# Turning the tokens of single batches with VectorE blocks and small transfers instead of TensorE

## The chip, the core and the metric

The kernel runs on one core of a Trainium2 chip. The metric is the device time of one execution in microseconds. Before the change the median of three runs is 2033.48 us (2031.84 to 2034.04).

The engines go by the profile's names: PE is TensorE, DVE is VectorE, ACT is ScalarE, POOL is GpSimd, SP is SyncE. SP and POOL matter here only as queues that issue transfers; each queue issues in program order, and each engine runs its instructions in program order.

## The reference

```python
# x: 8 batches x 4096 tokens x 192 channels; 8 heads of 24 channels, 7 taps
w    = softmax(weight, axis=-1)                    # 8 x 7
conv = sum over k of w[head, k] * x[token - 6 + k] # causal, per head
# mixing over tokens: w_tok1 4096x256, w_tok2 256x4096
h = relu(conv.T @ w_tok1) @ w_tok2
u = conv + h.T
# mixing over channels: w_ch1 192x1536, w_ch2 1536x192
out = u + relu(u @ w_ch1) @ w_ch2
```

The kernel does each matrix product as three products of a high and a low part (`hi*hi + hi*lo + lo*hi`), so each operand has to be split: the high part is a rounded copy, the low part is the value minus the high part.

## The kernel before, in words

The batches are worked in five groups, `[0], [1], [2, 3], [4, 5], [6, 7]`: two single batches, then three pairs. A batch's 4096 tokens are worked in 8 tiles of 512 (four columns `j` of 128). While group g's tiles go through the channel products, the background prepares group g+1: its convolution on DVE (line 659, six taps behind a first tap on ACT, line 657) and its first token product on PE (lines 761 for singles, 765 to 767 for pairs), whose sum over all 4096 tokens has to be complete before the next group's first tile can be formed.

One tile runs so on PE:

- **channel 1** (`channel1_mm`, line 1012): 6 steps of 18 matmuls. Each reads the turned tokens (channels on partitions), `own_hi` and `own_lo`. ACT (1051) and DVE (1052) turn each result into the pair `hh`, `hl`.
- **token mix** for the *next* tile (`mix2`, lines 909 and 910 for singles, 912 to 914 for pairs). DVE adds the results to the convolved tokens in `u` (922, 923; for pairs 927).
- **channel 2** (lines 1086, 1087): 4 columns of 24 matmuls, each closed by two DVE adds (1092, 1093) into `osb`.

The next tile's tokens stand token by row and have to be turned before its channel 1. For **single** batches PE does it, in the middle of channel 2 (`transposed`, line 945: 12 transposes of 128x128 against an identity, from a doubled copy of the tokens that ACT makes at line 924), and ACT (947) and DVE (948) split the result from PSUM. For **pairs** the work goes around PE: DVE turns each column in 32x32 blocks as soon as it is mixed (928) into a buffer `z` that takes the slot of `own_hi`; 16 transfers of 48 KB (`blocks_sent`, 961), eight from SP's queue and eight from POOL's, put the blocks in their places; and in the third column of channel 2, after its eighth of twelve steps, ACT and DVE split what arrived (`parted`, 974 and 976).

The order is set by a planner, `Background`. It keeps estimated clocks for PE and DVE. Each foreground step adds its estimate (`bg.fg(pe, dve)`), and background items are placed while the estimated DVE is not ahead of the estimated PE by more than a margin. Items also have gates: the first tap on a loaded chunk waits until the load should have landed. Between `bg.hold()` and `bg.release()` the convolution's big loads and stores are kept back, so that the small transfers go ahead of them; `bg.behind` adds 5 us to what is released. Before a group's last tile, `bg.finish` writes out everything of the next group's preparation that is not yet placed; PE's remaining token product stands there, ahead of the last tile's channel 1.

## Time and profile before

| | us |
|---|---|
| median of three runs | 2033.48 |
| the profiled execution | 2034.48 |
| its span, first to last instruction | 2032.7 |
| PE busy | 2019.6 |
| DVE busy | 1452.2 |
| ACT busy | 761.7 |
| POOL busy | 220.3 |

In the trace the tiles of batch 0 take PE from 62 to 335 us, those of batch 1 to 608 us, and the rest are pairs. A tile is told by its first line-1012 matmul: batch 0's second tile starts at 101.66 us, its last at 305.04 us, batch 1's first at 335.04 and its last at 577.96 us. "Busy" of PE counts from an instruction's start to its modelled end, and matmuls overlap, so PE's cost of a stretch is read here from the start of one group of matmuls to the start of the next.

### The profile page before, as it was taken

To read this page: it belongs to the slowest core of one execution; us is meant where nothing else is said; L and a number is where in the kernel's file an instruction comes from. 1 tells how busy PE (TensorE), PEld (TensorE's weight loads), DVE (VectorE), ACT (ScalarE), POOL (GpSimd) and SP (SyncE) were. 2 spreads that over 40 slices of the span, in tenths; PEclk is the share of its full clock that TensorE was granted. 3 is DMA by queue.
4 is the path that set the end of the run, shared out by engine and by line. 5 is a ranking of instruction groups with operands and counts; after the bars stand their busy time and mean duration, and the time that the engine had idled before them with its cause. 6 is when DMAs were issued, how large, how long until landed. Compare 5 with 4: busy or idle time off the path is not lost.

```text
span 2032.7 us, 42017 instructions
## 1 busy us (share of the span) xinstructions
PE 2019.6 (99%) x17435; PEld 1857.9 (91%) x17435; DVE 1452.2 (71%) x2877; ACT 761.7 (37%) x1305; POOL 220.3 (11%) x383
## 2 busy tenths in 40 slices
PE   9999999999999999999999999999999999999999
PEld 9789999999999898999999999999999999999998
DVE  7899998999659998756986689545555545555554
ACT  4575544444433434233333334233222332233322
POOL 0100000000011011101111110111111011111110
PEclk9999999999999999999999999999999999999999
DMA  9855346454434567324654334533222233233310
GB/s 304 294 158 170 119 155 201 152 163 157 142 117 131 165 200 202 101 82 130 169 162 114 106 107 137 150 89 84 71 61 57 71 84 84 76 84 84 84 48 17
DMA packets 289230, 258.39 MB, mean 127 GB/s; under 512 B 209360, under 2 KB 238544, under 8 KB 289040
## 3 DMA queue, kind: packets, MB, share of 16 engines
q1 hardware_dynamic: 265120, 168.00, 29.2%
q0 software_dynamic: 23920, 87.71, 14.0%
q8 instruction: 138, 2.26, 0.5%
q14 instruction: 52, 0.43, 0.1%
HBM read 146.60 MB, written 71.30 MB: 107 GB/s over the span
## 4 chain that ended last, share of the span: by engine, by line
PE 88%; DVE 5%; DMA 4%; SPq 1%; ACT 1%; issue 1%; POOL 0%; DVEq 0%; ACTq 0%
PE ps_x L1012 36%; PE ps_x L1086 17%; PE ps_x L1069 15%; PE ps_x L1087 8%; PE ps_x L912 2%; PE ps_a L765 2%; DVE xc L659 2%; PE ps_a L767 2%; PE ps_a L766 2%; PE ps_x L914 2%; PE ps_x L913 2%; PE ps_x L909 1%; PE ps_x L945 1%; PE ps_a L761 1%; DMA dec_raw<-in_moe_w_ch_dram 1%; DVE hl L1052 1%
## 5 line engine op out<-in xcount | busy, mean ns | idle before, releaser
L1051 ACT ACTIVATE hh<-ps_x 128x512 fp32r<-128x512 f32 x756 | 410.9, 596 | 743.3 <-PE ps_x L1012 743.2
L1052 DVE SCALAR_TENSOR_TENSOR hl<-ps_x,hh 128x512 fp32r<-128x512 f32 x756 | 484.5, 685 | 198.0 <-ACT hh L1051 196.6
L1086 PE MATMUL ps_x<-w,hh 128*128 128x384 f32 x1872 | 538.3, 359 | 0.1
L1087 PE MATMUL ps_x<-w,hl 128*128 128x192 f32 x1872 | 468.6, 250 | 0.0
L1012 PE MATMUL ps_x<-other,w_hi 64*128 64x512 f32 x1728 | 450.2, 389 | 1.0 <-DVE osb L1093 0.9
L659 DVE SCALAR_TENSOR_TENSOR xc<-raw,cw,xc 128x384 f32<-128x384 f32 (+1 forms) x768 | 389.2, 562 | 9.8 <-ACT xc L657 9.8
L1087 PEld LDWEIGHTS ps_x<-w,hl 128*128 128x128 f32 x1872 | 357.4, 191 | 0.0
L1086 PEld LDWEIGHTS ps_x<-w,hh 128*128 128x128 f32 x1872 | 351.4, 188 | 0.7 <-DVE hl L1052 0.7
L1012 PEld LDWEIGHTS ps_x<-other,w_hi 64*128 64x128 f32 x1728 | 314.0, 184 | 32.6 <-issue 1.3
L1012 PE MATMUL ps_x<-own_hi,w_hi 64*128 64x512 f32 x1440 | 333.6, 393 | 1.6 <-DVE hl L1052 0.9
L1069 PE MATMUL ps_x<-w,hh 64*128 64x384 f32 x2304 | 329.8, 355 | 0.0
L1012 PE MATMUL ps_x<-own_hi,w_lo 64*128 64x512 f32 x1440 | 325.4, 387 | 0.0
L1012 PE MATMUL ps_x<-own_lo,w_hi 64*128 64x512 f32 x1440 | 325.3, 386 | 0.0
L1069 PE MATMUL ps_x<-w,hl 64*128 64x192 f32 x2304 | 294.0, 247 | 0.0
L1012 PEld LDWEIGHTS ps_x<-own_hi,w_hi 64*128 64x128 f32 x1440 | 209.6, 184 | 37.8 <-issue 6.2
L1012 PE MATMUL ps_x<-other,w_lo 64*128 64x512 f32 x864 | 242.0, 386 | 0.0
L1012 PEld LDWEIGHTS ps_x<-own_hi,w_lo 64*128 64x128 f32 x1440 | 215.2, 184 | 29.1 <-DVE w_lo L212 0.5
L1012 PEld LDWEIGHTS ps_x<-own_lo,w_hi 64*128 64x128 f32 x1440 | 215.4, 184 | 28.1
L1069 PEld LDWEIGHTS ps_x<-w,hl 64*128 64x128 f32 x2304 | 229.0, 188 | 1.1 <-DVE hl L1052 0.2
L1069 PEld LDWEIGHTS ps_x<-w,hh 64*128 64x128 f32 x2304 | 225.2, 184 | 0.9
L1012 PEld LDWEIGHTS ps_x<-other,w_lo 64*128 64x128 f32 x864 | 159.0, 184 | 16.0
L1092 DVE TENSOR_TENSOR osb<-ps_x,u 128x192 f32<-128x192 f32 x156 | 55.4, 355 | 144.3 <-PE ps_x L1087 143.7
(143 smaller groups left out, 2153.2 us busy)
## 6 DMA issues: line engine op xcount, KB each, us to landing
raw<-in_x_dram SPq DMA_DIRECT2D x56, 672.0 KB, 7.5
t<-t2d SPq DMA_DIRECT2D x64, 512.0 KB, 5.4
out_dram<-osb POOLq DMA_DIRECT2D x63, 384.0 KB, 4.6
u<-xcd SPq DMA_DIRECT2D x62, 384.0 KB, 6.6
xcd<-xc POOLq DMA_DIRECT2D x28, 768.0 KB, 7.5
t<-t1p SPq DMA_DIRECT2D x32, 512.0 KB, 4.9
other<-own_hi SPq DMA_DIRECT2D x192, 48.0 KB, 2.1
other<-own_hi POOLq DMA_DIRECT2D x192, 48.0 KB, 2.0
```

The lines of the kernel that those rows point to most:

```text
L659: nc.vector.scalar_tensor_tensor(out=dst, in0=src, scalar=cw[:, h, k:k + 1], in1=dst, op0=ALU.mult, op1=ALU.add)
L765: nc.tensor.matmul(out=ps, lhsT=wh, rhs=xh, start=a, stop=False)
L766: nc.tensor.matmul(out=ps, lhsT=wh, rhs=xl, start=False, stop=False)
L767: nc.tensor.matmul(out=ps, lhsT=wl, rhs=xh, start=False, stop=z)
L912: nc.tensor.matmul(out=ps[:, :n], lhsT=wh, rhs=hh, start=a, stop=False)
L1012: nc.tensor.matmul(out=ps, lhsT=w1[w][rows, c, p * P:(p + 1) * P], rhs=t[h][v][rows, c], start=n == 0, stop=n == len(prods) - 1,)
L1051: nc.scalar.activation(out=h["hh", f], in_=ps, func=AF.Relu)
L1052: nc.vector.scalar_tensor_tensor(out=h["hl", f], in0=ps, scalar=0.0, in1=f32(h["hh", f]), op0=ALU.max, op1=ALU.subtract)
L1069: nc.tensor.matmul(out=ps[:, :m], lhsT=h[part, f][ks, ts], rhs=w2[ks, f, :m], start=n == 0 and part == "hh", stop=z and part == "hl",)
L1086: nc.tensor.matmul(out=ps[:, :2 * D], lhsT=h["hh", f][:, ts], rhs=w2[:, f, :], start=n == 0, stop=False)
L1087: nc.tensor.matmul(out=ps[:, :D], lhsT=h["hl", f][:, ts], rhs=w2[:, f, :D], start=False, stop=z)
L1092: nc.vector.tensor_tensor(out=rows(osb[:, j]), in0=rows(ps[:, :D]), in1=tokens(u, i)[:, j], op=ALU.add)
```

## The change

For the turns to tiles 3 to 8 of batch 0 and to all eight tiles of batch 1 (14 turns) the single batches take the way of the pairs, with some differences:

- `u` holds a tile's two copies one behind the other (`flat`), not alternating by 64 channels. DVE adds both as before and then turns the mixed copy by 32x32 blocks into `z` (new line 938). The copy on ACT (924), the 12 transposes on PE (945) and the split from PSUM (947, 948) are gone for these turns.
- The 16 transfers write into the slot of `own_lo` itself. Rows 64 to 127 get the same channels as rows 0 to 63, so every block is sent twice.
- `parted_single`: ACT writes the high part in the tokens' true order (998); DVE subtracts in place (1004), and the low part stays in the order in which the blocks arrived. Channel 1 reads it through a permuted view, in runs of 32 elements.
- Loads and stores of the convolution are held from channel 1's third step on, and a held load of a single batch now counts the 5 us of `bg.behind`.

```diff
             else:
                 mark("load", q2, part)
+                done["load", q2, part] += bg.behind
...
+            elif turned is not None and nb == 1:
+                two, one = flat(u)[:, j, 0], flat(u)[:, j, 1]
+                nc.vector.tensor_tensor(out=one, in0=ps[:, :D], in1=one, op=ALU.add)
+                nc.vector.tensor_tensor(out=two, in0=ps[:, D:2 * D], in1=one, op=ALU.add)
+                nc.vector.transpose(
+                    out=turned[:, :D // QB, j * QB:(j + 1) * QB], in_=two.rearrange("p (n e) -> p n e", e=QB)
+                )
+                bg.dve += 380
...
+        if nb == 1:
+            other = own_tile("lo")
+            blocks = z[:, :D // QB].rearrange("p (c n) t -> p n c t", n=NQ // 2)
+            home = other
...
                 queue.dma_start(
-                    out=f32(other[q * QB:(q + 1) * QB, 1, :, i * P:(i + 1) * P]), in_=blocks[i * QB:(i + 1) * QB, q]
+                    out=f32(home[q * QB:(q + 1) * QB, :, i * P:(i + 1) * P]),
+                    in_=blocks[i * QB:(i + 1) * QB, q % (2 * nb)],
                 )
...
+    def parted_single(lo):
+        own = own_tile("hi")
+        for c in range(ND):
+            v = f32(lo[:, c])
+            nc.scalar.copy(
+                out=own[:, c].rearrange("p (j i e) -> p j i e", i=NQ, e=QB),
+                in_=v.rearrange("p (i j e) -> p j i e", i=NQ, e=QB),
+            )
+            bg.fg(0, 700, 0)
+            blocks = "p (i j e) -> p i j e"
+            nc.vector.tensor_tensor(
+                out=lo[:, c].rearrange(blocks, i=NQ, e=QB), in0=v.rearrange(blocks, i=NQ, e=QB),
+                in1=f32(own[:, c]).rearrange("p (j i e) -> p i j e", i=NQ, e=QB), op=ALU.subtract,
+            )
+        own = own, lo.rearrange("p c (i j e) -> p c j i e", i=NQ, e=QB)
+        return [(own, own)]
...
         for p in range(NP):
+            if p == hold:
+                bg.hold()
...
-                if turn and pairs:
-                    bg.hold()
+                by_blocks = turn and (pairs or ahead)
                 if ahead:
-                    h = channel1(abc[i])
+                    h = channel1(abc[i], (0 if pairs else 2) if by_blocks else None)
...
+                    if by_blocks:
+                        other = blocks_sent(z, len(GROUPS[nxt[0]]))
+                        bg.release()
                 if ahead:
                     product2(i, h, u, osb, half[0])
-                if turn and not pairs:
+                if turn and not by_blocks:
                     abc = transposed(loaded[1])
...
-                        if turn and pairs:
+                        if by_blocks:
                             made = []
-                            channel2(i, h, u, osb, half[1], ((half[1][0], 7), lambda: made.extend(parted(other))))
+                            split = parted if pairs else parted_single
+                            channel2(i, h, u, osb, half[1], ((half[1][0], 7), lambda: made.extend(split(other))))
```

The planner's sums change with it, so the background stands elsewhere. The first place is DVE at the end of channel 2 of batch 0's seventh tile, where `bg.finish` writes out the rest of batch 1's preparation. `xc` and `raw` are the convolution's result and input, `h` is the finished first token product. Before:

```order
L1092 TENSOR_TENSOR osb<-ps_x,u 128x192
L1093 TENSOR_TENSOR osb<-ps_x,osb 128x192
L948 TENSOR_TENSOR own_lo<-ps_x,own_hi 128x512 x3
L1092 TENSOR_TENSOR osb<-ps_x,u 128x192
L1093 TENSOR_TENSOR osb<-ps_x,osb 128x192
L1092 TENSOR_TENSOR osb<-ps_x,u 128x192
L1093 TENSOR_TENSOR osb<-ps_x,osb 128x192
L382 SCALAR_TENSOR_TENSOR h_486<-ps_a_759,h_486 128x192
```

With the change:

```order
L1139 TENSOR_TENSOR osb<-ps_x,u 128x192
L1140 TENSOR_TENSOR osb<-ps_x,osb 128x192
L659 SCALAR_TENSOR_TENSOR xc_3164<-raw_2855,cw,xc_3164 128x8x24 x12
L1004 TENSOR_TENSOR own_lo<-own_lo,own_hi 128x512 x3
L659 SCALAR_TENSOR_TENSOR xc_3164<-raw_2855,cw,xc_3164 128x8x24 x2
L1139 TENSOR_TENSOR osb<-ps_x,u 128x192
L1140 TENSOR_TENSOR osb<-ps_x,osb 128x192
L659 SCALAR_TENSOR_TENSOR xc_3164<-raw_2855,cw,xc_3164 128x8x24 x2
L659 SCALAR_TENSOR_TENSOR xc_3164<-raw_3151,cw,xc_3164 128x8x24 x10
L1139 TENSOR_TENSOR osb<-ps_x,u 128x192
L1140 TENSOR_TENSOR osb<-ps_x,osb 128x192
L659 SCALAR_TENSOR_TENSOR xc_3164<-raw_3151,cw,xc_3164 128x8x24 x14
```

Before, batch 1's convolution was complete a tile earlier and PE's last 16 line-761 matmuls stood inside the seventh tile's token mix; now 14 taps stand behind the tile's last add, and those 16 matmuls stand between the tile's channel 2 and the last tile's channel 1.

The second place is DVE at the end of channel 2 of batch 1's seventh tile, where the rest of the first pair's preparation is written out. `xhl` is the split convolution result that PE multiplies, `t` and `other` the split first token weight (`other` is a spare buffer). Before:

```order
L749 TENSOR_TENSOR xhl<-xc_5281,xhl 128x768
L1092 TENSOR_TENSOR osb<-ps_x,u 128x192
L1093 TENSOR_TENSOR osb<-ps_x,osb 128x192
L733 TENSOR_TENSOR other<-other 128x2x256
L749 TENSOR_TENSOR xhl<-xc_5281,xhl 128x768
L733 TENSOR_TENSOR other<-other 128x2x256
L749 TENSOR_TENSOR xhl<-xc_5281,xhl 128x768
L382 SCALAR_TENSOR_TENSOR h_486<-ps_a_3724,h_486 128x384
```

With the change (the last four pairs of lines 734 and 750 are cut to one):

```order
L1139 TENSOR_TENSOR osb<-ps_x,u 128x192
L1140 TENSOR_TENSOR osb<-ps_x,osb 128x192
L659 SCALAR_TENSOR_TENSOR xc_5938<-raw_5923,cw,xc_5938 128x16x24 x20
L750 TENSOR_TENSOR xhl<-xc_5148,xhl 128x768
L734 TENSOR_TENSOR t_6207<-t_6207 128x2x256
L750 TENSOR_TENSOR xhl<-xc_5938,xhl 128x768
```

Twenty taps now stand behind the last add, and in front of five of the six splits that PE's remaining product of 72 matmuls (48 before) waits for; the first of the six was made earlier. From the end of this flush on, DVE's rows are the same in both kernels to the end of the program.

More of the change, by code (lines that the diff above doesn't have):

```diff
@@ L949, in transposed, with blocks_sent @@
         return [(own, own)]
-    def blocks_sent(z):
-        other = sp.tile([P, 2, ND, TT], F32R, name="other")
-        blocks = z.rearrange("p (c n) t -> p n c t", n=NQ)
+    def blocks_sent(z, nb):
+        if nb == 1:
+            other = own_tile("lo")
+            blocks = z[:, :D // QB].rearrange("p (c n) t -> p n c t", n=NQ // 2)
+            home = other
+        else:
+            other = sp.tile([P, 2, ND, TT], F32R, name="other")
+            blocks = z.rearrange("p (c n) t -> p n c t", n=NQ)
+            home = other[:, 1]
         for k in range(NQ):
@@ L1037, in conv_mixer_kernel, with channel1 @@
     order = [p + h * NP for p in range(NP) for h in range(2)]
-    def channel1(t):
+    def channel1(t, hold):
         h = {}
@@ L1243, in conv_mixer_kernel @@
                     first_channel2(u, osb, half[0])
-                if turn and pairs:
-                    z = up.tile([P, ND * NQ, P], F32, name="own_hi")
-                    mix2(*nxt, *loaded, turned=z)
-                    other = blocks_sent(z)
-                    bg.release()
-                elif turn:
+                if turn:
                     if gi == 0 and nxt[0] == 0:
                         bg.require(("t2", nxt[1] // 2, nxt[1] % 2))
-                    mix2(*nxt, *loaded)
+                    z = up.tile([P, ND * NQ, P], F32, name="own_hi") if by_blocks else None
+                    mix2(*nxt, *loaded, turned=z)
                     mixed[0] = nxt[1]
+                    if by_blocks:
+                        other = blocks_sent(z, len(GROUPS[nxt[0]]))
+                        bg.release()
                 product2 = channel2 if turn or last and q + 1 == NT and i + 1 == nb else channel2_halves
```

12 lines of the change are left out of this document (10 added, 2 removed).

## The prediction

> **What bounds the kernel now.** I read the page's shares and slices first, then the chain of waits, then the busy times by stretch over the single batches.
>
> ```profile
> span 2032.7 us, 42017 instructions
> PE 2019.6 (99%) x17435; PEld 1857.9 (91%) x17435; DVE 1452.2 (71%) x2877; ACT 761.7 (37%) x1305; POOL 220.3 (11%) x383
> DVE  7899998999659998756986689545555545555554
> PE 88%; DVE 5%; DMA 4%; SPq 1%; ACT 1%; issue 1%; POOL 0%; DVEq 0%; ACTq 0%
> ```
>
> PE is busy 99% of the span and is 88% of the chain: whatever leaves PE shortens the time, as long as nothing makes PE wait. The last row is DVE's busy tenths in 40 slices: in the first twelve, where the change acts, it stands at 7 to 9 for the most part.
>
> ```profile
> 275.00:300.00 25.00, 24.90 (x179) 22.92 (x177) 24.79 (x52) 9.19 (x20) 0.55 (x1) 1.00 0.27 94
> 550.00:575.00 25.00, 25.00 (x170) 24.92 (x169) 14.16 (x30) 9.29 (x17) 2.60 (x5) 1.00 0.38 127
> ```
>
> Each row is a stretch; the columns are its length, then busy time of PE, PEld, DVE, ACT, POOL, the granted clock (1.00, full), DMA share and GB/s. At the end of batch 0 DVE is busy 24.79 of 25 us and PE still 24.90; at the end of batch 1 DVE has 11 us to spare in 25. So DVE is nearly a second bound while batch 0 runs, and only the planner's early finish of the convolution keeps it off PE.
>
> **What PE sheds.** PE's rows of one single tile, from the first channel-2 matmul to the next channel 1, and the same stretch in a tile that turns a pair by blocks:
>
> ```profile
> 349.86 0.36 PE L1086 MATMUL ps_x<-w,hh 128*128 128x384 f32 x1
> 356.69 1.47 PE L945 MATMUL ps_x<-ident,u 128*128 128x128 f32 x12
> 357.92 0.42 PE L1086 MATMUL ps_x<-w,hh 128*128 128x384 f32 x1
> 365.04 0.97 PE L1012 MATMUL ps_x<-own_hi,w_hi 64*128 64x512 f32 x6
> ...
> 594.72 0.33 PE L1086 MATMUL ps_x<-w,hh 128*128 128x384 f32 x1
> 608.44 0.49 PE L1012 MATMUL ps_x<-own_hi,w_hi 64*128 64x512 f32 x1
> ```
>
> The 12 transposes hold PE from 356.69 to 357.92, 1.23 us. The whole stretch takes 15.18 us with them and 13.72 without, 1.46 less: changing operations costs something too. I take 1.35, between the two. Fourteen turns give 18.9 us (17.2 to 20.4). One stall goes as well:
>
> ```profile
> PE ps_x L1012 <- DVE osb L1093: 0.9, 1, 0.9
> ```
>
> It is DVE's backlog before batch 0's seventh tile, where the order now has fewer taps: 0.9 us. Gain: 19.8.
>
> **What the new way costs.** First the rows for its operations (groups by line and shape; of the transfers, the issue durations as min/median/max in ns):
>
> ```profile
> L928 DVE STREAM_TRANSPOSE own_hi<-u 128x384 f32<-128x384 f32 x96 | 55.6, 579 | 3.3
> L961 SPq DMA_DIRECT2D other<-own_hi x192: 589/597/1987, 596.8 to 1970.1; - x192
> L961 POOL DMA_DIRECT2D other<-own_hi x192: 548/548/586, 597.4 to 1969.2; - x192
> L976 DVE TENSOR_TENSOR own_lo<-other,own_hi 128x512 fp32r<-128x512 f32 x72 | 45.5, 687 | 40.6 <-ACT own_hi L974 37.4 <-DMA t<-t2d 3.2
> ```
>
> The turn of 192 columns isn't in the trace. It lies between half the 384-column turn, 0.29, and the whole, 0.58; I take 0.41, near the middle: 1.6 us more of DVE per tile. The subtraction is priced by the pairs' row, 0.69, and takes the place of one of the same shape; ACT sheds four copies, which nothing waits for once they are gone. Eight issues of 0.60 on SP run beside eight of 0.55 on POOL: 4.8 us until the last is out. Behind them in SP waits the held convolution load.
>
> **When the turned tokens are ready.** The rows of a token mix and turn, single and pair:
>
> ```profile
> 317.50 0.44 PE L909 MATMUL ps_x<-h,t 128*128 128x384 f32 x1
> 318.24 1.29 DVE L1052 SCALAR_TENSOR_TENSOR hl<-ps_x,hh 128x512 fp32r<-128x512 f32 x2 [0.69 <-ACT hh L1051]
> 319.45 0.35 DVE L922 TENSOR_TENSOR u<-ps_x,u 128x192 f32<-128x192 f32 x1
> 319.86 0.36 PE L1086 MATMUL ps_x<-w,hh 128*128 128x384 f32 x1
> 320.11 0.35 DVE L922 TENSOR_TENSOR u<-ps_x,u 128x192 f32<-128x192 f32 x1
> ...
> 596.12 0.58 DVE L928 STREAM_TRANSPOSE own_hi<-u 128x384 f32<-128x384 f32 x1
> 604.05 1.67 ACT L974 CAST own_hi<-other 128x512 fp32r<-128x512 f32 x3 [12.43 <-DMA other<-own_hi]
> 604.71 1.90 DVE L976 TENSOR_TENSOR own_lo<-other,own_hi 128x512 fp32r<-128x512 f32 x3 [2.24 <-ACT own_hi L974]
> ```
>
> Count from the first mix matmul. DVE begins the adds at 1.95 (319.45 − 317.50) and needs 0.66 + 0.41 a column, so the last turn ends at 6.2, up to 6.9 with two taps ahead. From the end of the last turn (596.70) to ACT's first copy a pair took 7.35 us; the same 16 issues give 13.6 to 14.3 here, and all three copies are out 1.67 later, at 15.2 to 15.9. The next channel 1 begins at 2.36 (319.86 − 317.50) + 13.72 = 16.1. So it fits, with as little as 0.2 us to spare; cost 0. DVE, in order, waits at the subtractions as it does for pairs (2.24 us), with the last adds and taps behind it; that costs nothing as long as DVE's work for a tile plus this wait stays under PE's time for it.
>
> **Where the order makes PE wait.** The rows that price the two flushes:
>
> ```profile
> 255.55 0.67 PE L761 MATMUL ps_a<-xc,t 128*128 128x192 f32 x3
> 256.87 0.60 PE L945 MATMUL ps_x<-ident,u 128*128 128x128 f32 x4
> 272.73 2.06 DVE L659 SCALAR_TENSOR_TENSOR xc<-raw,cw,xc 128x192 f32<-128x192 f32 x6
> 274.70 1.28 DVE L1052 SCALAR_TENSOR_TENSOR hl<-ps_x,hh 128x512 fp32r<-128x512 f32 x2
> 305.14 0.36 DVE L1092 TENSOR_TENSOR osb<-ps_x,u 128x192 f32<-128x192 f32 x1 [2.66 <-PE ps_x L1087]
> 305.81 0.61 DVE L382 SCALAR_TENSOR_TENSOR h<-ps_a,h 128x192 fp32r<-128x192 f32 x2
> 500.66 3.26 DVE L659 SCALAR_TENSOR_TENSOR xc<-raw,cw,xc 128x384 f32<-128x384 f32 x6
> 503.83 0.35 DVE L1092 TENSOR_TENSOR osb<-ps_x,u 128x192 f32<-128x192 f32 x1
> 569.49 0.36 PE L765 MATMUL ps_a<-xhl,t 128*128 128x384 f32 x1
> 577.96 0.96 PE L1012 MATMUL ps_x<-own_hi,w_hi 64*128 64x512 f32 x6
> L749 DVE TENSOR_TENSOR xhl<-xc,xhl 128x768 fp32r<-128x768 f32 x48 | 45.6, 950 | 3.2 <-ACT xhl L745 3.2
> ```
>
> A tap takes 0.33 us for a single (272.73 to 274.70, six) and 0.53 for a pair (500.66 to 503.83); a column's two adds 0.67 (305.14 to 305.81); four line-761 matmuls 1.32; twelve of the pairs' product 2.1 (8.47 for 48).
>
> *End of batch 0.* In its seventh tile DVE's last turn ends at 6.9. Behind it the new order has 52 taps (17.1), eight adds (2.7) and three subtractions (1.8): 28.5. PE has the mix (2.36), channel 2 (13.72) and 16 line-761 matmuls between (5.3): 21.4. The next 16 need the last tap, so PE waits 7.1. The second half of the input is loaded behind the block issues, which may hold DVE a little and which no row prices; I add 0.5, 1 at the upper end, and take 7.6. It can't be under the 14 last taps and the adds, 5.3.
>
> *End of batch 1.* The last adds wait for the last channel-2 matmul and end 0.7 later; 20 taps are 10.6, the split 0.95. PE meanwhile has one group of twelve, 2.1. It waits 10.1, and no less, since the taps start as early as they can. After that its groups (2.1) take longer than the split that each needs (0.95), so nothing more is lost.
>
> Sum: −18.9 − 0.9 + 7.6 + 10.1 = **−2.1 us**. The profiled execution took 2034.48, 1.8 over its span and 1.0 over the median; against the median it gives **2031.4**. With the bounds of its terms, 2027.6 (−20.4 − 0.9 + 5.3 + 10.1) to 2036 (1.7 less gain, 0.5 more at the first flush, 2 us of lag at the second).
>
> [...] The low part is now read in runs of 32 floats. The nearest row is a matmul that reads runs of 24 against one that reads 192 in a row (min/median/max in ns), and below them two groups of channel 1 by start:
>
> ```profile
> L521 PE MATMUL ps_x<-x,band x64: 326/326/430, 13.2 to 46.0; 128*128 128x192 f32 x64
> L452 PE MATMUL ps_a<-xc,t x96: 326/326/430, 25.6 to 51.5; 128*128 128x192 f32 x96
> ...
> 270.48 0.87 PE L1012 MATMUL ps_x<-own_lo,w_hi 64*128 64x512 f32 x6
> 271.17 0.88 PE L1012 MATMUL ps_x<-own_hi,w_hi 64*128 64x512 f32 x6
> ```
>
> The first two agree at 326, so I price the read at 0. But they move 192 columns in 326 ns, while six of channel 1's matmuls of 512 columns are through in 0.69 us (270.48 to 271.17), 0.115 each: at that rate no row shows a broken read. Half the rate would cost 36 x 0.115 = 4.1 us a tile, 58 in all. [...]
>
> **The rivals.**
> - *DVE falls behind within the tiles.* The waits at the subtractions (2.24) aren't covered in batch 0, where DVE is busy over 24 us in 25. Six tiles then carry them and the dearer turn (4 x 0.17) to the first flush, 17 us, and half as much reaches the second: 26 more than forecast at worst (2057), half of it likelier, **2044**. For it: 24.79. Against: the order has placed fewer taps in each of these tiles. It decides once DVE's backlog at a token mix passes about 1 us, since then channel 1 waits for its high part.
>   [...]
> - *The blocks land late* among batch 0's weight and token loads. Each turn that is 1 us late costs that; at 10 turns **2041**.
> - *The permuted read is slow*: half rate, **2089**; a tenth slower, 2037.
> - *The flushes cost nothing* and all of 19.8 stays: **2014**. Against it: 14 and 20 taps stand in front of matmuls that need them.
>
> **How the numbers follow.** The forecast has 0.52, DVE behind 0.27, late blocks 0.08, the slow read 0.07, the free flushes 0.06. About 4 us (0.2%) is what a measurement can tell from no change, 2029.4 to 2037.6. Of the forecast's 0.52, 0.12 lies under it and 0.40 within; late blocks and DVE behind by little put 0.06 within, free flushes 0.06 below, the rest above: faster 0.18, same 0.46, slower 0.36. The range takes the forecast's bounds and most of DVE behind, 2027 to 2050; the forecast's own is 2027.6 to 2036.
>
> **What would show it.** In the changed profile: PE's stretch from channel 2 to channel 1 near 13.7 us in single tiles; line-762 matmuls idle about 7 us once for DVE line 659; the pairs' product idle about 10 us for line 750, once; six `own_lo` matmuls of line 1057 still through in 0.69 us; no idle time at line 1057 for ACT line 998. Idle time at 1057 in most tiles means DVE behind or late blocks, told apart by whether the turns or the landings are late. Longer `own_lo` rows make the read guilty; no idle at 762 and 768 makes the flush sums wrong.

## The result and the profile after

The changed kernel takes 2056.88 us (median of four runs, 2056.20 to 2057.68) against 2033.76 for the kernel before beside it: a ratio of 1.0116, with a 95% interval from 1.0098 to 1.0133. The change makes the kernel slower by 23 us; 2031.4 was forecast. The profiled spans are 2055.9 and 2032.7 us.

The head of the page of the changed kernel (busy times, DVE's busy tenths in 40 slices, the chain's shares by engine and line):

```profile
span 2055.9 us, 42360 instructions
PE 2017.9 (98%) x17267; PEld 1856.2 (90%) x17267; DVE 1470.0 (72%) x2933; ACT 744.6 (36%) x1249; POOL 281.0 (14%) x495
DVE  8798987899977999856985689555555555455554
PE 77%; DVE 11%; DMA 5%; SPq 3%; ACT 2%; issue 1%; POOL 0%; ACTq 0%; POOLq 0%
```

PE has 1.7 us less to do than before and ends 23.2 us later, so PE waits. DVE's share of the chain went from 5% to 11%.

Where the time went, read from PE's timeline, from the first matmul of one stage to the first of the next, over the stretch from batch 0's second tile to the end of the single batches (101.66 to 577.96 us before, 101.08 to 596.37 after):

| stage of PE (us) | before | after | difference |
|---|---|---|---|
| channel 1, 14 tiles | 177.5 | 188.8 | +11.2 |
| token mix | 34.2 | 34.7 | +0.5 |
| channel 2 with the transposes | 211.1 | 194.6 | −16.5 |
| idle ahead of batch 1's last token product | 0 | 9.4 | +9.4 |
| that product's matmuls (lines 761/762) | 19.4 | 21.8 | +2.5 |
| the pairs' product, its idle time included | 34.2 | 46.0 | +11.8 |
| sum | 476.3 | 495.3 | +19.0 |

The rest of the program, the pairs, is longer by 4.8, and the stretch begins 0.6 earlier: 23.2 in all. Five readings carry this table.

**The two idles** stand where the prediction put them. PE's waits, costliest first (in all, times, longest):

```profile
PE ps_a L767 <- DVE xhl L750: 10.4, 1, 10.4
PE ps_a L762 <- DVE xc L659: 9.4, 1, 9.4
```

**The granted clock falls during them.** Stretches of 5 us around the first idle (from 297.4 to 306.76 us) and the second (574.1 to 584.44); the number ahead of the last two is the granted clock:

```profile
295.00:300.00 5.00, 2.37 (x17) 2.14 (x15) 4.20 (x13) 3.08 (x6) 0.00 (x0) 1.00 1.05 349
300.00:305.00 5.00, 0.00 (x0) 0.00 (x0) 4.96 (x17) 0.00 (x0) 0.76 (x1) 0.60 0.38 135
305.00:310.00 5.00, 3.24 (x10) 3.25 (x11) 1.70 (x6) 0.00 (x0) 0.55 (x1) 0.50 0.39 158
310.00:315.00 5.00, 5.00 (x30) 4.68 (x30) 0.55 (x2) 0.66 (x2) 0.00 (x0) 0.88 0.00 0
...
580.00:585.00 5.00, 0.56 (x2) 0.56 (x3) 5.00 (x10) 1.35 (x2) 0.91 (x1) 0.50 0.00 0
585.00:590.00 5.00, 5.00 (x23) 5.00 (x22) 2.44 (x4) 1.36 (x2) 1.99 (x3) 0.73 0.90 290
```

The clock goes to 0.50 some 3.6 and 3.4 us into the idles and is still there when work comes back, for about 4.5 and 3.3 us. The matmuls behind the first idle take 7.6 us instead of 5.3, those behind the second 11.9 instead of 10.5. Each time it stays at 0.50 for 10.2 us (from 301.0 and 577.5 us). In the late pair below, idles of 1.5 and 2.1 us with half a microsecond of matmuls between them were followed by 3.4 us at 0.50.

**Channel 1 stalls.** DVE and ACT around the start of batch 1's first tile (channel 1 from 343.19 us), each row a start, a busy time, and in brackets the wait ahead of it:

```profile
341.32 1.66 ACT L998 CAST own_hi<-own_lo 128x512 fp32r<-128x512 f32 x3 [11.32 <-DMA own_lo<-own_hi]
341.98 1.90 DVE L1004 TENSOR_TENSOR own_lo<-own_lo,own_hi 128x512 fp32r<-128x512 f32 x3 [2.34 <-ACT own_hi L998]
343.79 0.35 DVE L1139 TENSOR_TENSOR osb<-ps_x,u 128x192 f32<-128x192 f32 x1
344.45 2.20 DVE L659 SCALAR_TENSOR_TENSOR xc<-raw,cw,xc 128x384 f32<-128x384 f32 x4
345.64 1.09 ACT L1098 ACTIVATE hh<-ps_x 128x512 fp32r<-128x512 f32 x2 [2.66 <-PE ps_x L1057]
346.57 0.35 DVE L1139 TENSOR_TENSOR osb<-ps_x,u 128x192 f32<-128x192 f32 x1
347.23 2.20 DVE L659 SCALAR_TENSOR_TENSOR xc<-raw,cw,xc 128x384 f32<-128x384 f32 x4
349.34 1.28 DVE L1099 SCALAR_TENSOR_TENSOR hl<-ps_x,hh 128x512 fp32r<-128x512 f32 x2
350.08 1.55 PE L1057 MATMUL ps_x<-own_hi,w_hi 64*128 64x512 f32 x6 [0.30 <-DVE hl L1099]
```

DVE stands 2.34 us at the subtractions and leaves them at 343.88, after channel 1 has begun. Behind them, in order, come two columns' adds and eight taps, and only then `hl`, at 349.34, though ACT's `hh` was there at 346.2. PE then has to wait until `hl` has freed the PSUM buffers (`ps_x`) of its first products. Of the 14 turns' channel 1, seven take 12.72 to 12.74 us and seven 13.2 to 14.6; together the stalls are 8.9 us.

**Channel 1 is also longer where nothing stalls.** PE's first groups of channel 1 in a tile without stalls, of the changed kernel:

```profile
538.68 0.97 PE L1057 MATMUL ps_x<-own_hi,w_hi 64*128 64x512 f32 x6
539.48 0.86 PE L1057 MATMUL ps_x<-own_hi,w_lo 64*128 64x512 f32 x6
540.18 0.87 PE L1057 MATMUL ps_x<-own_lo,w_hi 64*128 64x512 f32 x6
540.88 0.86 PE L1057 MATMUL ps_x<-own_hi,w_hi 64*128 64x512 f32 x6
541.58 0.86 PE L1057 MATMUL ps_x<-own_hi,w_lo 64*128 64x512 f32 x6
```

And the fourth to the sixth group of such a tile in the kernel before:

```profile
505.69 0.84 PE L1012 MATMUL ps_x<-own_hi,w_hi 64*128 64x512 f32 x6
506.37 0.84 PE L1012 MATMUL ps_x<-own_hi,w_lo 64*128 64x512 f32 x6
507.05 0.84 PE L1012 MATMUL ps_x<-own_lo,w_hi 64*128 64x512 f32 x6
```

From the fourth group to the fifth it is 0.70 us instead of 0.68, and the groups that read the high part are slower too: 12.73 us a tile instead of 12.48, 3.5 us for 14.

**A pair is late once.** POOL issues the blocks of one pair with a pause in the middle (2.39 us), and PE waits 1.5 us for ACT's copy:

```profile
1756.90 1.67 POOL L988 DMA_DIRECT2D other<-own_hi  x3 [16.70 <-DVE own_hi L949]
1760.96 2.71 POOL L988 DMA_DIRECT2D other<-own_hi  x5 [2.39 <-issue]
1768.77 1.66 ACT L1019 CAST own_hi<-other 128x512 fp32r<-128x512 f32 x3 [17.68 <-DMA other<-own_hi]
```

That tile's channel 1 then takes 16.30 us instead of 12.4, with a second idle of 2.1 us and the 3.4 us at half clock in it. Together this is 5.4 us, more than the 4.8 by which the rest of the program grows; the other tiles differ by up to 1.4 us, in both directions.

### The profile page after: what moved, and what is told of

It is laid out like the page before. It is cut to its first block, busy times and chain, and to the rows that moved or that the text cites. A ratio compares the mean times of both kernels' runs of the same rounds, so it can differ in the third digit from the quotient of the medians.

```text
span 2055.9 us, 42360 instructions
## 1 busy us (share of the span) xinstructions
PE 2017.9 (98%) x17267; PEld 1856.2 (90%) x17267; DVE 1470.0 (72%) x2933; ACT 744.6 (36%) x1249; POOL 281.0 (14%) x495
## 4 chain that ended last, share of the span: by engine, by line
PE 77%; DVE 11%; DMA 5%; SPq 3%; ACT 2%; issue 1%; POOL 0%; ACTq 0%; POOLq 0%
PE ps_x L1057 34%; PE ps_x L1116 16%; PE ps_x L1133 12%; PE ps_x L1134 5%; DVE xc L659 3%; SPq L988 2%; DVE hl L1099 2%; PE ps_x L925 2%; PE ps_a L767 1%; PE ps_a L766 1%; PE ps_a L768 1%; PE ps_x L927 1%; PE ps_x L926 1%; DMA dec_raw<-in_moe_w_tok_dram 1%; DMA raw<-in_x_dram 1%
## 5 line engine op out<-in xcount | busy, mean ns | idle before, releaser
L1057 PE MATMUL ps_x<-own_hi,w_hi 64*128 64x512 f32 x1440 | 343.8, 398 | 5.8 <-DVE hl L1099 2.0
L1057 PE MATMUL ps_x<-own_lo,w_hi 64*128 64x512 f32 x1440 | 331.4, 389 | 0.0
L1057 PE MATMUL ps_x<-own_hi,w_lo 64*128 64x512 f32 x1440 | 330.7, 388 | 0.0
L1116 PE MATMUL ps_x<-w,hl 64*128 64x192 f32 x2304 | 299.2, 247 | 0.0
L1057 PEld LDWEIGHTS ps_x<-own_hi,w_hi 64*128 64x128 f32 x1440 | 214.0, 184 | 46.9 <-DVE hl L1099 9.4
L1057 PEld LDWEIGHTS ps_x<-own_hi,w_lo 64*128 64x128 f32 x1440 | 219.9, 184 | 27.8 <-DVE w_lo L212 0.5
L1057 PEld LDWEIGHTS ps_x<-own_lo,w_hi 64*128 64x128 f32 x1440 | 220.3, 185 | 27.0
L1116 PEld LDWEIGHTS ps_x<-w,hl 64*128 64x128 f32 x2304 | 239.3, 188 | 0.9
L1116 PEld LDWEIGHTS ps_x<-w,hh 64*128 64x128 f32 x2304 | 235.8, 184 | 0.9
L988 POOL DMA_DIRECT2D other<-own_hi x192 | 104.7, 553 | 428.6 <-DVE own_hi L949 330.2
```

What stands on the lines that cost most here:

```text
L988: queue.dma_start(out=f32(home[q * QB:(q + 1) * QB, :, i * P:(i + 1) * P]), in_=blocks[i * QB:(i + 1) * QB, q % (2 * nb)],)
L1057: nc.tensor.matmul(out=ps, lhsT=w1[w][rows, c, p * P:(p + 1) * P], rhs=t[h][v][rows, c], start=n == 0, stop=n == len(prods) - 1,)
L1116: nc.tensor.matmul(out=ps[:, :m], lhsT=h[part, f][ks, ts], rhs=w2[ks, f, :m], start=n == 0 and part == "hh", stop=z and part == "hl",)
```

## The experiments

Ratios are against runs of the kernel before on the same chip, with their 95% interval. The medians of the kernel before were 2031.6 to 2033.0 us.

### Where the taps stand, and the clock

`sums_old` puts the planner's sums back and keeps all 14 turns:

```diff
-                bg.dve += 380
...
-            bg.fg(0, 700, 0)
+            bg.fg(440, 600)
```

> All 14 turns by blocks, but the planner's sums as before (no 380 ns of DVE a column, 440 ns of PE and 600 of DVE at each of the three splits). In the written order no tap is left behind the last add of either seventh tile. Theory 'DVE is short in batch 0': the two idles (9.39 and 10.36 us) and the slow restarts behind them (2.3 and 1.4) vanish, 23.5 in all, but batch 0 has no room on DVE, so its six turns, each dearer by 1.6 us of turn and some 2 us of wait at the subtractions, come back as stalls in channel 1, 10 us or more: about 2043. Rival 'the planner's sums alone': the tiles stay as they are and the 23.5 us are gone: 2033.4.

Measured: 2054.02 us, 1.0107 (1.0092 to 1.0122). The idles have shrunk to 1.4 and 1.1 us, and nearly all of their time comes back in channel 1: 206.9 us for the 14 tiles, 18.1 more than in the changed kernel and 29.4 more than before; single tiles take up to 19.2. An estimated 3 to 5 of the 18.1 are slow clock again: the mean granted clock is 0.98 over the 212 us from 101.16 to 313.20, and 1.00 over batch 0's stretch in the kernel before. Neither number was right; the theory was nearer in kind, and its price for the tiles was too low by nearly half. So taking the idles away doesn't take the loss away: DVE's lateness can be paid at the flushes or in channel 1.

`busy_flush` keeps PE busy during the idles:

```diff
         def finish():
+            if gi in (1, 2):
+                ps = ps_x.tile([P, TT], F32, name="ps_x")
+                for k in range(80 if gi == 1 else 88):
+                    nc.tensor.transpose(out=ps[:, k % TJ * P:(k % TJ + 1) * P], in_=ident, identity=ident)
             bg.finish(gi)
```

> The changed kernel with PE kept busy at the two idles: 80 and 88 transposes of the identity into a spare buffer stand on PE where each group's remaining preparation is written out, 8.2 and 9.0 us by the before kernel's 1.23 us for twelve, less than the idles (9.39 and 10.36). They compute nothing that is used. Theory 'an idle PE loses its clock': the granted clock stays 1.00 through both places and the matmuls behind them take 5.3 and 10.5 us in place of 7.6 and 11.9: 3.7 us less, 2053.2. Rival 'those matmuls are slow for another cause' (their operands just written): 2056.9.

Measured: 2056.06 us, 1.0118 (1.0103 to 1.0133). At the first place it does what was expected: the clock stays at 1.00 and the product takes 5.40 us (the transposes have line 850):

```profile
296.52 8.89 PE L850 MATMUL ps_x<-ident 128*128 128x128 f32 x80
306.43 5.47 PE L762 MATMUL ps_a<-xc,t 128*128 128x192 f32 x32 [1.01 <-DVE xc L659]
```

At this place the slow restart is shown. At the second PE still stood idle for 3.7 us ahead of DVE's split, and the matmuls behind it start 0.32 us apart up to 586.31 us, from there 0.17, so a slow restart is there all the same. And what PE gains at the first is not in the end time: DVE begins the split 241.11 us after batch 1's first tile begins, in the changed kernel 240.24 (the starts of channel 1 are 340.65 and 343.19 us). DVE sets that time, and PE, there earlier, waits for it.

### One batch alone

`only_b1` turns by blocks only for batch 1's eight tiles, `only_b0` only for batch 0's six; the others are turned by PE as before.

```diff
+    def by(gi, q):
+        return gi > 0
...
-                by_blocks = turn and (pairs or ahead)
+                by_blocks = turn and (pairs or ahead and by(*nxt))
```

That is `only_b1`; in `only_b0` the function returns `gi == 0 or gi > 1`. The lines left out give the turns by PE their old token layout back.

> Blocks only for the eight turns to batch 1's tiles; batch 0 as before, the planner's new sums kept. Theory 'DVE is short in batch 0': batch 0 as before (seventh tile's end without idle), eight channel 2 shorter by 1.33 us, eight channel 1 longer by 0.25, up to 4 us of stalls in the first tiles of batch 1, no second idle of 10 us (no tap is left in the written order): 2025 to 2030. Rival 'a turn by blocks costs more than it saves in any single tile': 2034 or more.

> Blocks only for the six turns to batch 0's tiles; batch 1 as before. Theory: the first idle and its slow restart stay (11.7 us), channel 1 of six tiles is longer by 5 in all, channel 2 shorter by 8.0, the second idle is gone: 2042. Rival 'the second idle comes from batch 0's delay': it stays too, 2054.

Measured: 2037.95 us, 1.0027 (1.0016 to 1.0038) for batch 1 alone, 2047.75 us, 1.0073 (1.0057 to 1.0090) for batch 0 alone. The first contradicts the theory, and its rival holds: there is no second idle of 10 us (2.4 remain), but six of batch 1's eight channel 1 stall by 0.4 to 2.2 us, and the blocks land later, a median of 9.2 us from the last turn to ACT's first copy against 7.4 in the changed kernel. For batch 0 the first idle stays (8.6 us) and the second is gone, so that the second idle is no heritage of batch 0 alone, nor made by batch 1 alone. Apart the two cost 5 and 15 us, together 23.

### What holds DVE up

`dve_extra` gives the kernel before the turn's DVE work without anything that waits for it:

```diff
+    spare = const.tile([P, D], F32, name="spare")
+    nc.vector.memset(spare, 0.0)
...
                 nc.scalar.copy(out=one, in_=two)
+                if (gi, q) not in ((0, 0), (0, 1)):
+                    nc.vector.transpose(
+                        out=spare.rearrange("p (n e) -> p n e", e=32),
+                        in_=spare.rearrange("p (n e) -> p n e", e=32),
+                    )
```

> The kernel before, with one added DVE instruction behind each column's adds for the 14 later turns of the single batches: a 32x32 block turn of a spare 192-column tile onto itself, which nothing reads (56 instructions of 0.38 us, 21 us of DVE in all). PE's work, the planner's sums and the order of all else stay. Theory 'DVE has no room': batch 0 and the first tiles of batch 1 take most of their 10 x 1.5 us as stalls in channel 1: 8 to 15 us longer, 2040 to 2047 by the first median. Rival 'the turn itself is hidden, and only the wait at the subtractions makes DVE late': within 3 us of before.

Measured: 2033.59 us, 1.0007 (0.9998 to 1.0016). The rival's first half holds: 56 more DVE instructions, 12.6 us more of DVE busy time over the stretch (the change adds 17.3), and 1 us for PE. So the turn's work alone is hidden; that the wait is what makes DVE late, this run can't show. The stretch in one row (its length; busy time and instructions of PE, PEld, DVE, ACT and POOL; granted clock; DMA's share and GB/s), of the kernel before:

```profile
101.66:577.96 476.30, 475.14 (x3570) 439.36 (x3569) 420.48 (x911) 223.99 (x415) 30.47 (x47) 1.00 0.50 158
```

Of this kernel:

```profile
100.01:577.40 477.39, 475.71 (x3570) 438.33 (x3569) 433.03 (x967) 223.89 (x415) 30.18 (x47) 1.00 0.50 158
```

Of the changed one:

```profile
101.08:596.37 495.29, 471.27 (x3401) 428.70 (x3400) 437.82 (x967) 207.22 (x359) 91.88 (x159) 0.98 0.57 174
```

`sub_late7` moves only the three subtractions (now in `low_parts`), from the third column of channel 2 to the eighth step of the fourth:

```diff
+    AT = 7
...
+                if low and at and (j, n) == (at[0][0] + 1, AT):
+                    low_parts()
```

> The changed kernel with only the three DVE subtractions of a single turn moved back, from the third column of channel 2 (eighth step) to the fourth column (eighth step); ACT's copies stay. The written order then leaves 10 taps in place of 14 behind batch 0's seventh tile and 2 in place of 20 behind batch 1's. Theory 'DVE stands still at the subtractions (20.3 us in 10 turns) and is late for channel 1 by that': the first pair of hl in the stalled tiles comes 2 us sooner, channel 1's stalls of 9 us in all fall to 4 or less, the idles to about 7 and 3: 2040. Rival 'DVE is late by its own longer work': channel 1's stalls stay, only the idles shrink: 2046.

Measured: 2047.05 us, 1.0073 (1.0058 to 1.0088): about 9 us better than the changed kernel, and at the rival's number. Channel 1 gains 2.9 us, and the pairs' product with its idle time 6.6 (39.4 against 46.0), since only 2 taps are left there; the first idle stays at 9.2. DVE now stands 2.2 us at the subtractions in all, where it stood 21.7. In batch 1 the stalls are nearly gone with that (0.6 us instead of 4.2; seven tiles run at 12.7), as the theory says; in batch 0 they stay (5.1 instead of 4.8), as the rival says. The place of the taps changed with the edit, so the split between the two isn't clean in this run.

`b1_sums_late` has both: blocks for batch 1 alone, the sums of before, the subtractions in the fourth column (fifth step).

> Blocks for batch 1's eight turns alone, the planner's sums as before, the subtractions in the fourth column (fifth step). DVE's taps then stand nearly as in the kernel before, with the last two tiles of batch 1 almost free of them. Theory 'blocks pay where DVE has room': tiles five to eight gain 1.08 us each, the first four lose some of it to stalls; no idle of more than 2 us before the pairs: 2026 to 2031. Rival 'blocks cost more than they save in every tile': 2034 to 2040.

Measured: 2044.45 us, 1.0061 (1.0046 to 1.0076), 6 us worse than `only_b1`. Both theories for batch 1 alone had named a time below before's, and both fell. They had counted on room on DVE. Its rows in the kernel before, which the prediction had not read for this stretch, from batch 0's second tile to its last, over batch 1's first five tiles, and over its sixth and seventh, in which the turns to the last two are made:

```profile
101.66:305.04 203.38, 202.22 (x1523) 186.18 (x1522) 190.38 (x458) 113.33 (x202) 8.08 (x12) 1.00 0.48 151
335.04:503.51 168.47, 168.47 (x1271) 156.69 (x1270) 160.19 (x316) 71.98 (x139) 13.81 (x21) 1.00 0.54 171
503.51:577.96 74.45, 74.45 (x550) 69.09 (x549) 45.66 (x88) 27.25 (x51) 6.69 (x11) 1.00 0.46 150
```

DVE is busy 94%, 95% and 61% (and 81% of batch 0's last tile, between the first two). With the taps where they were, most of batch 1 has no more room than batch 0.

`sub_pool` takes the subtractions off DVE altogether (`nc.gpsimd.tensor_tensor` for `nc.vector.tensor_tensor` in `parted_single`, 0 for 700 ns in the planner's sum); `sub_pool_old` also takes out the 380 ns a column; `sub_pool_b1` is that for batch 1 alone.

> The changed kernel with the three subtractions of a single turn on POOL in place of DVE, and 0 in place of 700 ns for each in the planner's sum; the planner then leaves no tap behind batch 1's seventh tile and fewer behind batch 0's. DVE no longer waits for the blocks. Theory 'the wait makes DVE late': the first hl of every tile comes near 3 us behind channel 1's start (4 to 7 in the changed kernel), channel 1's stalls come only from a low part that POOL makes later than DVE did (POOL's time for 128x512 is in no run so far; at twice DVE's 0.69 the last third comes some 2 us later), and the time falls below 2040. Rival 'the lag is handed on through turn, transfers and copy whoever subtracts': first hl stays late, 2045 or more.

> The same, and the planner's 380 ns a column taken out, so that the taps stand nearly as in the kernel before and none is left for either end. Theory 'the wait makes DVE late': both idles gone and the tiles without DVE stalls: 2030 or less if POOL's subtractions come in time, up to 2040 if each turn loses 0.5 to 1 us to them. Rival 'the lag is handed on': as with the sums put back before, 2050.

> The same for batch 1's eight turns alone. Theory: batch 0 as before the change, eight turns at 1.33 us gained and 0.25 lost, no DVE stall: 2024 to 2030 if POOL is in time. Rival: 2038 or more, as with DVE's subtractions (2038 and 2044).

Measured: 2059.08 us, 1.0133 (1.0116 to 1.0150); 2061.88, 1.0148 (1.0133 to 1.0163); 2046.99, 1.0073 (1.0058 to 1.0088). None is better than its nearest kernel with DVE's subtractions (2056.88; 2054.02; 2037.95 and 2044.45), and `sub_pool_old` is clearly worse. The idles are gone or small (1.5 us at most), but POOL needs twice DVE's time and PE waits for it; who waited for line 1004 in `sub_pool`, from the rows of that line:

```profile
L1004 POOL TENSOR_TENSOR own_lo<-own_lo,own_hi x42: 1268/1384/1727, 131.7 to 589.6; 128x512 fp32r<-128x512 f32 x42
  PEld ps_x L1057: 17.4, 19
  PE ps_x L1057: 10.5, 14
```

By the times the rival holds, and in `sub_pool` the first `hl` comes 5.1 to 9.2 us behind channel 1's start in 13 of the 14 tiles. But the low part that comes too late delays channel 1 itself and hides what DVE gained, so the run doesn't decide between the two. It shows how tight the turn is: with the low part some 2 us later, nearly every tile pays.

### The read

`perm_read` is the kernel before with the low part written and read in the blocks' order:

```diff
-            nc.vector.tensor_tensor(out=own[1][:, c], in0=ps, in1=f32(own[0][:, c]), op=ALU.subtract)
+            true, sent = "p (j i e) -> p j i e", "p (i j e) -> p j i e"
+            nc.vector.tensor_tensor(
+                out=own[1][:, c].rearrange(sent, i=4, e=32), in0=ps.rearrange(true, i=4, e=32),
+                in1=f32(own[0][:, c]).rearrange(true, i=4, e=32), op=ALU.subtract,
+            )
+        own = own[0], own[1].rearrange("p c (i j e) -> p c j i e", i=4, e=32)
```

> The kernel before with one change: DVE writes the low part of the single tiles in the blocks' order and channel 1 reads it permuted, in runs of 32; turns, copies and the planner stay. Theory 'the permuted read slows channel 1': every single tile's channel 1 goes from 12.55 to 12.80 us, 16 x 0.25 = 4 us: 2037.8. Rival 'something else in the changed kernel adds the 0.25': 2033.8, channel 1 at 12.55.

Measured: 2036.21 us, 1.0016 (1.0006 to 1.0025), channel 1 12.73 us in the single tiles instead of 12.48. The read costs what the changed kernel showed.

`pool_pad` was meant for POOL's pause (twelve memsets on a new tile of 32 bytes a partition). `pad32` and `pad64` put such a tile, of 32 and of 64 bytes, into the kernel before.

> The changed kernel with twelve tiny memsets on POOL at the start, which nothing reads. In the changed kernel POOL pauses once, 2.39 us between the third and fourth of a pair's eight block issues (1758.6 us), and channel 1 of the next pair waits some 3.5 us. Theory 'the pause belongs to a place in POOL's instruction stream': moved by twelve instructions it falls where POOL is idle, and 3.5 to 4 us are gone: 2053. Rival 'it belongs to the transfers or the moment': it stays: 2056.9.

> The kernel before with a tile of 32 bytes a partition allocated behind the identity, so that every later tile lies 32 bytes further. Nothing reads it. With the twelve POOL memsets on such a tile channel 1 took 12.70 us instead of 12.38 in all 48 pair tiles. Theory 'the address decides': channel 1 goes to 12.7 to 12.8 us in all tiles and the time to 2050. Rival 'the memsets did it': 2033, 12.4 to 12.5 us.

> The same with a tile of 64 bytes. If only the place within 64 bytes counts, channel 1 stays at 12.4 to 12.5 us and the time at 2033; if any shift does it, it is as with 32 bytes, 2050.

Measured: 2074.43 us, 1.0210 (1.0193 to 1.0228) for `pool_pad`, and one run each of 2053.68 and 2041.59 for `pad32` and `pad64`. The addresses decide: with every later tile 32 bytes further channel 1 takes 12.71 us in the pair tiles and 12.80 in the single ones, with 64 bytes 12.49 and 12.58, against 12.39 and 12.48. Which of the moved tiles matters isn't shown. The pause stayed in `pool_pad`, between the same two of POOL's transfers (the 410th and the 411th), so it doesn't belong to a place in POOL's instruction stream. It was there with 403 and more transfers on POOL, mostly in the pairs' last group, and absent with 355 to 379; in `sub_pool_old`, and with two of six taps left out (next section), it was shorter and elsewhere. Its cause stays open.

### DVE relieved, and the turns that pay

`before_less` and `after_less` leave out two of DVE's six taps in the convolution of batch 1 and of the first pair, so their output isn't the reference's:

```diff
-                    tap(q2, h, k)
+                    if gi > 2 or k > 2:
+                        tap(q2, h, k)
```

> The kernel before with two of the six DVE taps left out in the convolution of batch 1 and of the first pair (their output is not the reference's), so that DVE has some 50 us less to do while the single batches run. The control for the next one. PE bounds it as before: 2030 to 2033 in all theories, less only by the 0.9 us stall.

> The changed kernel with the same taps left out. In the written order no tap is left behind either seventh tile. Theory 'DVE's budget': with 50 us of it free, the tiles run without stalls, channel 1 at 12.73 us in nearly all of them, both idles gone; against the control 14 x 1.33 gained, 14 x 0.25 lost to the permuted read, some 3.5 lost to POOL's pause: 11 to 15 us faster than the control, 2017 to 2021. Rival 'the chain of turn, transfers, copy and subtraction hands a lag on whatever DVE has to do': channel 1 keeps half of its stalls and more, the gain over the control is under 8 us, 2024 or more.

Measured: 2035.68 us, 1.0016 (1.0006 to 1.0025), and 2040.07 us, 1.0033 (1.0020 to 1.0046). The control came out 3.7 us above before, not at it: its planner places the work otherwise, and PE has one wait of 2.9 us for DVE and one of 1.4. With DVE relieved the change still costs 4 us against this control, where it cost 23 with all taps; no idle ahead of the products is left. That is not the gain of 11 to 15 that the theory asked for, and channel 1 of the 14 tiles takes 201.3 us, longer than the changed kernel's 188.8: by the bounds of the expectation the rival holds. Five of eight tiles of batch 1 run at 12.73 to 12.96 us, but three of the 14 single tiles take 17 to 19 each, and there DVE and ACT stand 3 to 6 us for the convolution's input, whose loads are held and then issued behind the blocks (in the changed kernel ACT waits 1.2 us for them in all). SP, then ACT in the worst of them:

```profile
400.44 15.80 SPq L647 DMA_DIRECT2D raw<-in_x_dram  x4
416.92 2.13 ACT L657 ACTIVATE xc<-raw,cw 128x384 f32<-128x384 f32 x4 [5.62 <-DMA raw<-in_x_dram]
```

So the run removes one limit and meets another. The other eleven turns have stalls of 5.9 us, and the same eleven of the changed kernel 6.8: room on DVE takes the idles away, but hardly the stalls in channel 1.

`three` and `two` use blocks only where DVE is nearly free: for the turns to batch 1's first and last two tiles, and to the last two alone, with the planner's sums as before.

> Blocks only for three turns, the ones in the tiles where DVE has room before the change: to batch 1's first tile (5.4 us of DVE idle time in the tile that makes it) and to its last two (8.5 and 15.4); all other turns on PE, the planner's sums as before, so that DVE's taps stand as in the kernel before. Theory 'a turn by blocks pays where DVE has room': channel 2 shorter by 1.33 us and channel 1 longer by 0.25 for each of the three, no stall: 3.2 us less than before, a ratio of 0.9984. Rival 'blocks cost more than they save in every tile': 1.000 or more.

> Blocks for two turns alone, to the last two tiles of batch 1, made in tiles with 8.5 and 15.4 us of DVE idle time; the planner's sums as before. Each gains 1.33 and loses 0.25 us: 2.2 us less than before, ratio 0.9989. With three turns, of which the one to batch 1's first tile lost 2.2 us to stalls behind it and gained 1.4, the ratio was 0.9989; by the trace two should be 0.8 us better than three. Rival 'the gain of three came from chance in its runs': 1.000.

Measured: 2029.95 us, 0.9989 (0.9980 to 0.9998), and 2028.50 us, 0.9981 (0.9972 to 0.9990). The turn to batch 1's first tile loses as much as it gains (channel 1 14.07 us); the last two run clean, and `two` is the fastest kernel here, 3.5 us better than before. Both of these turns also have a part of the pairs' product between token mix and channel 1 (22.4 and 24.8 us from the one to the other), so room on DVE and time for the chain aren't told apart. In `two` DVE also waits at the subtractions, but nothing late is queued behind it:

```profile
529.57 1.90 DVE L1006 TENSOR_TENSOR own_lo<-own_lo,own_hi 128x512 fp32r<-128x512 f32 x3 [2.00 <-ACT own_hi L1000]
531.39 0.35 DVE L1141 TENSOR_TENSOR osb<-ps_x,u 128x192 f32<-128x192 f32 x1
535.15 0.36 DVE L1141 TENSOR_TENSOR osb<-ps_x,u 128x192 f32<-128x192 f32 x1 [2.16 <-PE ps_x L1136]
540.25 1.29 DVE L1101 SCALAR_TENSOR_TENSOR hl<-ps_x,hh 128x512 fp32r<-128x512 f32 x2 [4.34 <-ACT hh L1100]
```

## Why the prediction was wrong, step by step

- **What PE sheds** (−18.9, from 1.35 a turn): right. Channel 2 fell from between 15.0 and 15.2 us to 13.75 in the tiles without stalls; 16.5 remain of it over the 14 turns, since some stalls fall into channel 2. The 0.9 us stall went too: that tile's channel 1 is 12.74 us, before 13.44.
- **The turn's chain**: right in its sizes, wrong in its start. The turn takes 0.38 (0.41 taken), the blocks a median of 7.4 us from the last turn to ACT's copy (7.35; single turns up to 9.9), and in the tile quoted above the high part is complete 0.2 us ahead of channel 1, as worked out. But the prediction took the start of DVE's adds, 1.95 us behind the first mix matmul, from one tile (317.50). In the kernel before they begin so early in 3 of the 14 tiles that later make a turn; in the others it is 2.6 to 5.4, and in the changed kernel 2.4 to 4.3. The turn to batch 0's third tile, first before, then after (first mix matmul, first add, and in the changed kernel the last turn):

```profile
116.01 0.44 PE L909 MATMUL ps_x<-h,t2s 128*128 128x384 f32 x1
120.03 0.35 DVE L922 TENSOR_TENSOR u<-ps_x,u 128x192 f32<-128x192 f32 x1
...
115.41 0.44 PE L922 MATMUL ps_x<-h,t2s 128*128 128x384 f32 x1
119.44 0.35 DVE L936 TENSOR_TENSOR u<-ps_x,u 128x192 f32<-128x192 f32 x1
123.36 0.38 DVE L938 STREAM_TRANSPOSE own_hi<-u 128x192 f32<-128x192 f32 x1
```

  So the last turn ends 6.7 to 10.5 us behind the mix's start, not 6.2 to 6.9, and the 0.2 us to spare are used up. In six turns PE goes straight from the mix to channel 2, 16 to 17 us from the mix to the next channel 1: all six stall in channel 1. Of the other eight, where a token product or the first idle lies between (20 us and more), one does.
- **The step that failed** is this "it fits, ... cost 0" together with the sentence behind it: that DVE's wait at the subtractions "costs nothing as long as DVE's work for a tile plus this wait stays under PE's time for it". Both were priced at 0; the stalls cost 8.9 us in channel 1 and some 3 in channel 2 and the mix. What stands behind the wait counts, not only the sum: adds and taps stood in front of `hl`. And DVE's room was read from one stretch at the end of each batch (24.79 and 14.16 of 25), of which the second was the exception: but for batch 0's last tile (81%) DVE was at 94 to 95% until 503 us. Over the stretch it had 55.8 us free (476.30 − 420.48). The change takes 17.3 more of work (437.82 − 420.48) and 21.7 of standing at line 1004 (quoted below), and would make the stretch 15.4 shorter (the 18.9 that PE sheds, less 3.5 for the read): 54.4 of 55.8, of which 28.8 lay in batch 1's sixth and seventh tiles. That no order could have fitted this in isn't shown, and room isn't all: with the standing nearly gone (`sub_late7`), or taps left out (`after_less`, in the turns without a wait for loads), most of the stalls stayed. How they divide between the late start, the standing and the order behind it stays open.

```profile
L1004 DVE TENSOR_TENSOR own_lo<-own_lo,own_hi x42: 684/686/693, 131.9 to 569.3; 128x512 fp32r<-128x512 f32 x42
  ACT own_hi L998: 20.3, 10
  DMA t2d<-stage: 1.4, 1
```

- **The two flushes** (+7.6, +10.1): places and causes right, idles of 9.4 and 10.4, and 2.3 and 1.4 more for the slow restart, which had no term. In the first, DVE stood 1.4 us at the subtractions and 0.8 for a late first tap, where the sum had 0.5. (The matmuls counted there as 16 and 16 are 32 and 32 in the trace; eight, not four, take 1.32 us, so their times were right.) Putting the order back doesn't win the two back: `sums_old` takes most of them away and gains 3 us, which lies within the intervals.
- **The permuted read** at 0: wrong by 0.25 us a tile, 3.5 in all. The prediction's check, the six `own_lo` matmuls through in 0.69 us, was too coarse to see it: they take 0.70. `perm_read` measured 2% (12.73 us against 12.48).
- **The pairs** had no term: 5.4 us in the pair behind POOL's pause.
- **The rivals**: "DVE falls behind within the tiles" (0.27) is what happened in the mechanism: DVE is late at the token mix, and channel 1 pays. That its highest price, 2057, is the measured time is luck: it has the lateness carried to the flushes (17 us and half as much again), whose idles came out only 1.8 and 0.3 longer than forecast, while channel 1, channel 2 and the mix lost some 12, and the rest of the miss is the read, the slow clock and the pairs. The turn by PE was the cheaper one for the 14 turns together (by 23 us) and for each batch's turns alone (15 and 5), and the turn by blocks for the two to batch 1's last tiles (by 3.5, `two`).

## What to carry to other kernels

Before work is moved from the bound engine to another, read over all of the tiles that will have it, not in one, how late the other engine begins and how much room it has; here the one tile read was among the 3 earliest of 14, and the end of a batch was the least typical stretch. For each new wait, list what is queued behind it on its engine and who needs that first: here it was taps ahead of `hl` (which began 3.1 us after `hh` was there, in the tile quoted), and two turns with nothing late behind the wait cost nothing. And price an idle of the matrix engine with its restart (2.3 and 1.4 us here), and a pass that takes work off one place with the place where it comes back.

## What was not expected of the hardware

- The place of the tiles in SBUF changes the speed of channel 1's matmuls (64 rows by 512; in the kernel before two start within 0.01 us, the next two 0.23 us later): all later tiles 32 bytes further cost 0.32 us in 12.4 and 20 us in all, 64 bytes 0.10 us and 9 (one run each). A permuted read of one operand in three had the same look: all matmuls of the step slow down, 12.73 us for the 108 of a tile instead of 12.48.
- An idle of 9.4 us costs 2.3 us more behind it, at a granted clock of 0.50; 80 spare transposes in the idle keep the clock at 1.00 and take that away (5.4 in place of 7.6 us). Shorter idles had it too: 1.5 and 2.1 us in the late pair (0.50 for 3.4 us), and 3.7 us in `busy_flush` (matmuls 0.32 us apart instead of 0.17).
- POOL's subtraction of 128x512 takes 1.38 us, DVE's 0.69.
- In the changed kernel POOL paused once for 2.4 us between two transfers of one burst, for no reason that the profile shows.
